# Loading a quarter of one weight chunk in two loads of 64 rows by the lower eight DMA engines, in a one-token attention kernel

## The chip, the cores and the metric

The kernel runs on one core of one Trainium2 chip. The time is the device time of one execution in microseconds (us), as the median of several runs. Most runs of one kernel agree within 0.3% (20 runs of the kernel before: 288.07 to 289.18 us, median 288.77). Now and then an execution takes some per cent longer (one of the changed kernel's took 297.79 us); such runs, the slow state, are left out of the ratios.

Engines are named as in the profile: PE (TensorE matmul), PEld (its weight load), DVE (VectorE), ACT (ScalarE), POOL (GpSimd), SP (SyncE, which issues nearly all transfers here). Beside them are 16 DMA engines. The traces do not number them. "Lower" is the name for the eight that carry a load whose source has an outer dimension of 8, "upper" for the other eight.

## The reference

One token goes through attention with a cached window and then a gated MLP. Cut to what matters here:

```python
x: (1, 1, 640)   k_cache, v_cache: (1, 32, 32768, 192)   wq: (640, 6144)   wo: (6144, 640)
W = 4096                                  # the last 4096 keys of each of 32 heads
q = layernorm(x) @ wq                     # 32 heads of 192
scores = q . k[:, :, -W:, :] / sqrt(192); p = softmax(scores); o = p @ v[:, :, -W:, :]
h  = x + o @ wo
h2 = h + mlp(layernorm(h))                # w_in (640 x 1536), gelu, gate, w_out (768 x 640)
```

All data are bfloat16. Keys and values are 2 x 50 MB, wq and wo 7.9 MB each: 119 MB in all, each byte used once.

## The kernel before

All large transfers are issued from SP in one fixed order: wq (five chunks of 128 rows), then tiles of keys and values of 3 MB, wo in pieces of 960 KB in between, and last w_in (five chunks) and w_out (six). Six buffers hold wq and KV tiles; SP issues a transfer once its buffer is free. The parts that the change and the argument touch:

```python
wq_v = A_wq.rearrange("(c p i) n -> c p (i n)", c=DC, i=4)      # DC = 5 chunks of 128 rows x 6144
...
def dma_wq(i):
    t = kvp.tile([P, KVE], BF16, tag="kv", name="wq_t")
    for c in range(2 * i, min(2 * i + 2, DC)):
        load(t[:, (c % 2) * HD:(c % 2 + 1) * HD], wq_v[c])        # 128 partitions x 12 KB
    tiles[("wq", i)] = t
...
for gq in range(NP // 2):                     # 8 groups of 4 heads
    psv = sc_bank()[:, 0:2 * Dh] ...
    for c in range(DC):
        wc = wq_sb[c // 2][...]
        for a in range(2):
            nc.tensor.matmul(psv, lhsT=xn2[:, c, a, :], rhs=wc[:, gq, a, :, :], ...)
    nc.scalar.activation(out=q2[...], in_=psv, func=ACT.Copy, scale=scale)
free("kv", NWQ)                               # now the next transfers may be issued
```

One chunk of wq reaches 128 partitions from 32 source runs of 48 KB (four rows each), so each DMA engine moves two packets of 48 KB for it (the trace of the kernel before has 160 such packets for the five chunks).

## Time and profile before

| | before |
|---|---|
| median of 6 runs | 288.61 us (288.27 to 289.18) |
| span of the profiled run | 286.9 us |
| main DMA queue, share of 16 engines | 96.9% |
| PE, DVE busy | 63%, 53% |
| one 48 KB packet, median | 1.815 us |

The page of the kernel before: the DMA share and the rate in 40 slices of 7.2 us, then the queues (packets, MB, share of 16 engines' span).

```profile
span 286.9 us, 3349 instructions
DMA  8999999999999999999999999999999998999991
GB/s 315 425 425 425 439 441 432 414 436 440 434 439 432 434 432 439 397 436 439 439 439 434 432 439 439 400 439 432 432 428 465 439 425 373 453 439 413 429 368 45
q1 hardware_dynamic: 4202, 119.35, 96.9%
q8 instruction: 11, 0.18, 0.2%
```

The DMA engines are busy from the first slice to the last, at nearly one rate (a packet counts in the slice in which it starts, so single slices scatter). No compute engine is near that (PE 63%, DVE 53%). Beside the data, eleven 16 KB packets of instructions (0.95 to 1.04 us each in the packet records) run on the DMA engines.

The end of the chain of waits of the kernel before, that is of the work that ended last, followed back at each step to what it waited for (start us, us, what):

```profile
271.52 8.71 DMA w_in_sb<-in_B_w_in_dram
280.23 0.05 issue
280.27 0.50 PE sm_ps L461 x12
284.46 0.28 DVE o_sb L490
```

And PE's timeline there (start us, us, engine, line, operation, count; in brackets the idle time before it and what ended it):

```profile
275.67 0.90 PE L376 MATMUL attn_ps<-o_1961,wo_t 128*128 128x1 bf16 x30 [1.07 <-DMA wo_t<-in_A_wo_dram]
278.65 1.42 PE L461 MATMUL sm_ps<-hb_2005,w_in_sb 128*128 128x1 bf16 x48 [0.33 <-DVE st_2007 L457]
280.27 0.48 PE L461 MATMUL sm_ps<-hb_2005,w_in_sb 128*128 128x1 bf16 x12 [0.20 <-DMA w_in_sb<-in_B_w_in_dram]
```

The end of the kernel hangs on the landings of wo and w_in. A transfer has landed when the last of its 16 shares has, so it is the slowest of the 16 DMA engines that counts here (the last completion in the third row below, at 278.16, is the landing at 280.23 of the chain above, on another clock). The trace holds the time of each of the 16 completions. Three transfers of the kernel before, in us on a clock that starts with the first data packet (2.1 us behind the page's clock), first completion and then the 16 offsets from it:

```
wq, chunk 0     4.65 | .00 .04 .05 .12 .15 .17 .25 .26  .52 .55 .64 .65 .68 .75 .83 .87
k, tile 0      26.48 | .00 .03 .04 .05 .12 .15 .17 .26  .53 .55 .65 .66 .67 .75 .80 .82
w_in, chunk 4 274.65 | .00 .03 .03 .41 .61 .70 .71 .82 1.47 1.62 2.00 2.00 2.16 2.19 3.40 3.51
```

At the start there are two groups of eight. At the end two engines are 3.5 us behind the first, 1.2 us behind the third-last. The average engine is done at 276.00, the last at 278.16.

### The profile page before, as it was taken

The numbers are of one execution on the slowest core, as the hardware profiler recorded it, in microseconds if no ns is written. First come the engines' busy times: TensorE is split into PE (matmuls) and PEld (weight loads), VectorE is DVE, ScalarE is ACT, GpSimd is POOL, SyncE is SP. The second block draws the span as 40 slices with busy tenths as digits, with TensorE's granted clock in tenths as the row PEclk, the third lists the DMA queues.
The fourth block names the chain that finished last, engine by engine and source line by source line (L and its number), as shares of the span: only waits on it lengthen the run. The fifth ranks groups of instructions, "written<-read, shape, count | busy, mean of one in ns | idle before, by whom it ended". The sixth has DMA issues, their size and how long they took to land.

```text
span 286.9 us, 3349 instructions
## 1 busy us (share of the span) xinstructions
PE 181.3 (63%) x1432; PEld 82.6 (29%) x1432; DVE 152.6 (53%) x204; ACT 28.7 (10%) x103; POOL 2.4 (1%) x13
## 2 busy tenths in 40 slices
PE   1229947698387664957394737656394919954853
PEld 0004613334133221423142313322141303423552
DVE  6100088998383909292565629290838447922133
ACT  2001300111002010101010010201010100201300
POOL 3000000000000000000000000000000000000000
PEclk9999989999959796987979896979597796998575
DMA  8999999999999999999999999999999998999991
GB/s 315 425 425 425 439 441 432 414 436 440 434 439 432 434 432 439 397 436 439 439 439 434 432 439 439 400 439 432 432 428 465 439 425 373 453 439 413 429 368 45
DMA packets 4223, 119.56 MB, mean 417 GB/s; under 512 B 1007, under 2 KB 1008, under 8 KB 1456
## 3 DMA queue, kind: packets, MB, share of 16 engines
q1 hardware_dynamic: 4202, 119.35, 96.9%
q8 instruction: 11, 0.18, 0.2%
q14 instruction: 4, 0.03, 0.0%
q10 hardware_dynamic: 6, 0.00, 0.0%
HBM read 119.34 MB, written 0.00 MB: 416 GB/s over the span
## 4 chain that ended last, share of the span: by engine, by line
DMA 68%; PE 16%; DVE 13%; SPq 1%; issue 1%; ACT 0%
DMA k_t<-in_A_k_cache_dram 34%; DMA v_t<-in_A_v_cache_dram 24%; DVE k_t L277 10%; PE sc_ps L283 9%; DMA wq_t<-in_A_wq_dram 7%; PE sc_ps L251 5%; DMA w_in_sb<-in_B_w_in_dram 3%; DVE S L291 1%; SPq L60 1%; PE pv_143 L338 1%; PE sm_ps L306 0%; PE attn_ps L372 0%; PE sm_ps L479 0%; PE pv_145 L338 0%; PE sm_ps L359 0%
## 5 line engine op out<-in xcount | busy, mean ns | idle before, releaser
L283 PE MATMUL sc_ps<-k_t,ident_bf 128*128 128x512 bf16 x384 | 112.5, 456 | 59.6 <-DVE k_t L277 59.6
L277 DVE TENSOR_TENSOR k_t<-k_t,q_178 128x6144 bf16<-128x6144 bf16 x32 | 107.2, 3352 | 58.0 <-DMA k_t<-in_A_k_cache_dram 58.0
L283 PEld LDWEIGHTS <-ident_bf 128*128 128x128 bf16 x384 | 42.0, 113 | 119.1 <-issue 70.7
L251 PE MATMUL sc_ps<-wq_t,xn_122 128*128 128x384 bf16 x80 | 17.7, 384 | 13.3 <-DMA wq_t<-in_A_wq_dram 10.9
L291 DVE TENSOR_REDUCE S<-sc_ps 128x32 f32<-128x512 f32 x32 | 21.6, 676 | 1.3 <-PE sc_ps L283 1.3
L308 DVE TENSOR_TENSOR bias<-off,sm_ps 128x2 f32<-128x2 f32 x16 | 2.4, 152 | 24.5 <-PE sm_ps L306 24.5
L259 DVE TENSOR_SCALAR sp_f<-sm_ps 128x1 f32<-128x1 f32 x1 | 0.2, 159 | 28.4 <-PE sm_ps L257 28.4
L251 PEld LDWEIGHTS <-xn_122 128*128 128x128 bf16 x80 | 8.7, 110 | 21.9 <-issue 15.6
L314 ACT ACTIVATE E_119<-S,bias 128x64 bf16<-128x64 f32 x12 | 4.2, 360 | 71.9 <-DVE bias L308 71.9
L338 PE MATMUL pv_143<-v_t,E_121 128*4 128x384 bf16 x96 | 6.2, 388 | 4.8 <-DMA v_t<-in_A_v_cache_dram 4.8
L314 ACT ACTIVATE E_120<-S,bias 128x64 bf16<-128x64 f32 x10 | 3.5, 361 | 51.6 <-DVE bias L308 51.6
L314 ACT ACTIVATE E_121<-S,bias 128x64 bf16<-128x64 f32 x10 | 3.5, 360 | 50.4 <-DVE bias L308 50.4
L338 PE MATMUL pv_145<-v_t,E_119 128*4 128x384 bf16 (+1 forms) x128 | 5.7, 327 | 3.7 <-DMA v_t<-in_A_v_cache_dram 3.7
L338 PE MATMUL pv_145<-v_t,E_120 128*4 128x384 bf16 x96 | 4.9, 325 | 4.7 <-DMA v_t<-in_A_v_cache_dram 4.7
L306 PE MATMUL sm_ps<-gm,ones_f 1*128 1x2 f32 x32 | 6.3, 263 | 2.3 <-DVE gm L301 2.3
L338 PEld LDWEIGHTS <-E_119 128*4 128x4 bf16 (+1 forms) x224 | 4.9, 91 | 8.8 <-issue 7.1
L301 DVE TENSOR_REDUCE gm<-sm_ps 1x2 f32<-1x128 f32 x16 | 4.4, 276 | 5.6 <-PE sm_ps L299 5.4
L306 PEld LDWEIGHTS sm_ps<-gm,ones_f 1*128 1x128 f32 x32 | 4.9, 190 | 8.1 <-DVE gm L301 3.5
L253 ACT ACTIVATE q_178<-sc_ps 128x384 bf16<-128x384 f32 x8 | 3.9, 490 | 29.8 <-PE sc_ps L251 29.8
L338 PEld LDWEIGHTS <-E_121 128*4 128x4 bf16 x160 | 3.3, 87 | 11.5 <-issue 10.4
L338 PEld LDWEIGHTS <-E_120 128*4 128x4 bf16 x160 | 3.2, 82 | 8.8 <-issue 7.5
L299 PE MATMUL sm_ps<-ident_f,m 128*1 128x128 f32 x16 | 5.0, 310 | 0.0
(151 smaller groups left out, 94.7 us busy)
## 6 DMA issues: line engine op xcount, KB each, us to landing
k_t<-in_A_k_cache_dram SPq DMA_DIRECT2D x15, 3072.0 KB, 32.2
v_t<-in_A_v_cache_dram SPq DMA_DIRECT2D x15, 3072.0 KB, 40.3
wq_t<-in_A_wq_dram SPq DMA_DIRECT2D x5, 1536.0 KB, 14.3
wo_t<-in_A_wo_dram SPq DMA_DIRECT2D x8, 960.0 KB, 32.5
w_in_sb<-in_B_w_in_dram SPq DMA_DIRECT2D x5, 384.0 KB, 23.2
k_t<-in_A_k_cache_dram SPq DMA_DIRECT2D x1, 1536.0 KB
v_t<-in_A_v_cache_dram SPq DMA_DIRECT2D x1, 1536.0 KB
w_out_sb<-in_B_w_out_dram SPq DMA_DIRECT2D x6, 160.0 KB, 5.5
```

The source lines that it names most:

```text
L60: eng.add_instruction(mybir.InstDMACopy(name=nc.get_next_instruction_name(), mode="Copy", queue="qSPDynamicHW", ins=eng.lower_ap_dma(in_, ...
L251: nc.tensor.matmul(psv, lhsT=xn2[:, c, a, :], rhs=wc[:, gq, a, :, :], start=(c == 0 and a == 0), stop=(c == DC - 1 and a == 1))
L253: nc.scalar.activation(out=q2[:, 2 * gq:2 * gq + 2, :], in_=psv, func=ACT.Copy, scale=scale)
L277: nc.vector.tensor_tensor(out=kc, in0=kc, in1=q2[:, t:t + 1, :].to_broadcast([P, JC, Dh]), op=ALU.mult)
L283: nc.tensor.matmul(psv, lhsT=ident_bf[:], rhs=k3[:, ch * JC:(ch + 1) * JC, n * G:(n + 1) * G], start=(n == 0), stop=(n == NT - 1))
L291: nc.vector.tensor_reduce(out=S[:, ch * JC:(ch + 1) * JC], in_=st[t]["ps"][ch], axis=AX.X, op=ALU.add)
L299: nc.tensor.transpose(out=mT[0:1, 0:P], in_=m[:], identity=ident_f[:])
L301: nc.vector.tensor_reduce(out=gm[:], in_=mT[0:1, 0:P].rearrange("o (g a s) -> o a g s", a=2, s=2), axis=AX.XY, op=ALU.max)
L306: nc.tensor.matmul(nb[:, 0:2], lhsT=ones_f[0:1, :], rhs=gm[:], start=True, stop=True)
L308: nc.vector.tensor_tensor(out=bias[:], in0=off[:], in1=nb[:, 0:2], op=ALU.subtract)
L314: nc.scalar.activation(out=E[:, :, a], in_=S[:], func=ACT.Exp, bias=bias[:, a:a + 1], accum_out=zq[q][:, a, b:b + 1])
L338: nc.tensor.matmul(pv_tiles[t % 2][p0:p0 + 2 * step, 0:step * Dh], lhsT=E[:, j:j + step, :].rearrange("p j a -> p (j a)"), rhs=vt[:, j * D ...
```

## The change

Its intent follows from that last row: the engines do not finish together, and a transfer that runs on the lower eight alone moves work from the upper ones to them. For the last 128 rows of wq, columns of three quarters of the heads come as before on all 16 engines. The last quarter (3 KB of each row) comes in two loads of 64 rows, both to partitions 0 to 63, side by side. A source whose outer dimension is 8 keeps the load on 8 engines. The matmuls of those heads then contract twice over 64 rows.

```diff
+    QCUT = 6 * 4 * Dh
 ...
-            load(t[:, (c % 2) * HD:(c % 2 + 1) * HD], wq_v[c])
+            if c < DC - 1:
+                load(t[:, (c % 2) * HD:(c % 2 + 1) * HD], wq_v[c])
+            else:
+                rows = A_wq[c * P:(c + 1) * P]
+                load(t[:, 0:QCUT], rows[:, 0:QCUT])
+                for h in range(2):
+                    load(t[0:HALF, None, h * HD + QCUT:(h + 1) * HD],
+                         rows[h * HALF:(h + 1) * HALF, QCUT:HD].rearrange("(a b) n -> a b n", a=8))
 ...
-    xn2 = const.tile([P, DC, 2, P], BF16)
+    xn2 = const.tile([P, DC + 1, 2, P], BF16)
 ... (x's last 64 values are put on partitions 0 to 63 once more: one matmul, two DVE operations)
-        for c in range(DC):
+        split = gq * 4 * Dh >= QCUT
+        nchunk = DC + 1 if split else DC
+        for c in range(nchunk):
+            n = HALF if split and c >= DC - 1 else P
 ...
-                nc.tensor.matmul(psv, lhsT=xn2[:, c, a, :], rhs=wc[:, gq, a, :, :],
+                nc.tensor.matmul(psv, lhsT=xn2[0:n, c, a, :], rhs=wc[0:n, gq, a, :, :],
```

No byte is added. Added work: four matmuls of 0.2 us in the q stage (72 of them in a row took 14.42 us in the kernel before), one tiny matmul, two small DVE operations (0.57 us for both there), two issues on SP (0.59 us each at the median).

More of the change, by code (lines that the diff above doesn't have):

```diff
@@ L229 @@
         nc.tensor.matmul(xc_ps[:, c:c + 1], lhsT=x_row[0:1, c * P:(c + 1) * P], rhs=ones_bf[0:1, 0:1], start=True, stop=True)
+    nc.tensor.matmul(xc_ps[0:HALF, DC:DC + 1], lhsT=x_row[0:1, D - HALF:D], rhs=ones_bf[0:1, 0:1], start=True, stop=True)
     x_pc = const.tile([P, 2, DC + 1], F32)
@@ L237 @@
     nc.vector.tensor_scalar(out=rstd1[:], in0=ln_rstd16(ln_nvar(mean1)), scalar1=1.0 / 16, scalar2=None, op0=ALU.mult)
-    for a in range(2):
-        nc.vector.tensor_scalar(out=xn2[:, :, a, :].rearrange("p c (g a s) -> p c a g s", a=2, s=2)[:, :, a],
-                                in0=x_pc[:, 0, 0:DC, None, None].to_broadcast([P, DC, HALF // 2, 2]),
-                                scalar1=mean1[:, 0:1], scalar2=rstd1[:, 0:1], op0=ALU.subtract, op1=ALU.mult)
+    for c0, c1, src in ((0, DC, x_pc[:, 0, 0:DC]), (DC, DC + 1, xc_ps[0:HALF, DC:DC + 1])):
+        n = src.shape[0]
+        for a in range(2):
+            nc.vector.tensor_scalar(out=xn2[0:n, c0:c1, a, :].rearrange("p c (g a s) -> p c a g s", a=2, s=2)[:, :, a],
+                                    in0=src[:, :, None, None].to_broadcast([n, c1 - c0, HALF // 2, 2]),
+                                    scalar1=mean1[0:n, 0:1], scalar2=rstd1[0:n, 0:1], op0=ALU.subtract, op1=ALU.mult)
     q2 = const.tile([P, NP, Dh], BF16)
@@ L247 @@
         psv = ps[:, 0:2 * Dh].rearrange("p (r d) -> p r d", r=2)
-        for c in range(DC):
+        split = gq * 4 * Dh >= QCUT
+        nchunk = DC + 1 if split else DC
+        for c in range(nchunk):
+            n = HALF if split and c >= DC - 1 else P
             wc = wq_sb[c // 2][:, (c % 2) * HD:(c % 2 + 1) * HD].rearrange("p (q a r d) -> p q a r d", a=2, r=2, d=Dh)
             for a in range(2):
-                nc.tensor.matmul(psv, lhsT=xn2[:, c, a, :], rhs=wc[:, gq, a, :, :],
-                                 start=(c == 0 and a == 0), stop=(c == DC - 1 and a == 1))
+                nc.tensor.matmul(psv, lhsT=xn2[0:n, c, a, :], rhs=wc[0:n, gq, a, :, :],
+                                 start=(c == 0 and a == 0), stop=(c == nchunk - 1 and a == 1))
         nc.scalar.activation(out=q2[:, 2 * gq:2 * gq + 2, :], in_=psv, func=ACT.Copy, scale=scale)
```

## The prediction

> **What bounds the kernel.** The DMA. The page gives 119.35 MB on the main queue, 96.9% of 16 engines' span, and 425 to 440 GB/s in most slices; a 48 KB packet takes 1.815 us (27.1 GB/s per engine) at its median in the packet records. The pieces of DVE and PE in the chain of waits (36.6 to 73 us) are not the limit: KV tiles keep landing every 7.26 us through that stretch, because transfers were queued 30 to 40 us ahead (DMA issues table). So the time is: first packet (3.3 us), the slowest engine's stream, and a tail. The timeline shows the tail hanging on landings: wo at 275.67, last w_in chunk at 280.27, w_out at 282.64, end 286.9.
>
> **The hidden imbalance.** The 16 completions of each transfer in the trace are not together. On the first wq chunk they spread over 0.87 us, in two groups of eight (0 to 0.26, 0.52 to 0.87). From then on the spread grows in steps of 1.4 to 1.55 us, one engine at a time, each when one of the eleven 16 KB packets of the "instruction" queue runs (0.95 to 1.04 us each; page, part 3). [...] Following the offsets, six of the first eight hit the later group, two the earlier, and a second round hits two of the later group again. At the end (last w_in chunks) offsets are 0, .01, .02, .39, .60, .68, .70, .80, 1.46, 1.60, 1.99, 1.99, 2.17, 2.18, 3.40, 3.56 us: by my tracking the early group ends at 1.6 or less, and the two stragglers are of the later group. Every landing is paid at 3.5.
>
> **Which half is which.** [...] The two-byte load on the Activation queue starts exactly when a packet of an early-group engine ends[...]. I take early = lower eight.
>
> **The change.** No bytes added or removed. wq's last chunk loses a quarter on the upper engines (24 KB each), which the lower ones get. Packet times read from the trace are close to linear (6 KB 0.235, 12 KB 0.465, 48 KB 1.815), so I estimate 0.35 us for 9 KB, 0.12 for 3 KB. Upper: 8 x 0.35 against 2 x 1.815, -0.85 us. Lower: plus 16 x 0.12, +1.05 us. New finish: upper 3.5 - 0.85 = 2.65, lower 1.6 + 1.05 = 2.65. Balanced: each late landing comes about 0.8 us earlier, and so do w_in, w_out and wo.
>
> Added: four matmuls in the q stage (4 x 0.2 us), one small matmul, two DVE operations before wq has landed, two DMA issues (0.6 us each). The q stage ends at 36.6 us; the transfers it frees are needed near 43 us. All off the critical path.
>
> **Prediction.** 288.6 - 0.8 = about 287.9 us, 80% range 287.2 to 289.0. Within 2%: 0.98.
>
> **What would show it.** Right: last w_in landing near 279.4, completion spread at the end about 2.7 instead of 3.5, 3 KB packets near 0.12 us, tile spacing still 7.26 us, same tail after w_in. First wq landings: the later group comes first in the last chunk.
>
> **What would make it wrong.** Early group is not the lower half (+1 us instead); 3 KB packets slow because eight engines write one half of the partitions (+1 us or so); instruction fetches falling on other engines with the ten added PE instructions; the queue running dry once at start through more transfers in flight.

The sharing out was to gain 0.8 us, which from 288.6 us gives about 287.9 us.

## The result, and the profile after

| | before | after |
|---|---|---|
| median | 288.77 us (20 runs, 288.07 to 289.18) | 289.48 us (10 runs; one of them slow, 297.79) |
| ratio of fast runs | | 1.0035, 95% interval 1.0023 to 1.0046 |
| span of the profiled run | 286.9 us | 287.5 us |

Of the ten runs of the changed kernel the nine fast ones have a median of 289.47 us. Ratios here and below are the mean time of one kernel's fast runs over that of the other's in the same rounds, so they are not quite the ratio of the medians. The change costs 0.7 us by the medians (1.0 us by the ratio) where 0.8 us were to be gained, and the result lies above the stated range. The loss is small, but the interval of the ratio leaves 1 out.

The page of the kernel after, the same lines:

```profile
span 287.5 us, 3362 instructions
DMA  7999999999999999999999999999999998999991
GB/s 308 431 388 405 424 433 410 424 465 434 438 438 431 440 417 424 428 423 438 438 438 447 431 438 438 390 433 438 438 430 455 431 433 380 456 438 409 439 376 63
q1 hardware_dynamic: 4442, 119.35, 97.1%
q8 instruction: 11, 0.18, 0.2%
```

The same megabytes, 240 packets more. The DMA share shows no hole, but the rate does: slices 3 and 4 (14.4 to 28.8 us, when the last chunk of wq comes) have 388 and 405 GB/s where the kernel before had 425 and 425 (with each packet shared out by time over the slices, 411 and 385 against 433 and 434). The engines are busy there and slow. A busy share alone would have hidden this.

The end of the chain of waits, and PE's timeline, after:

```profile
271.89 8.81 DMA w_in_sb<-in_B_w_in_dram
280.70 0.05 issue
280.75 0.49 PE sm_ps L475 x12
284.93 0.28 DVE o_sb L504
```

```profile
276.04 0.90 PE L390 MATMUL attn_ps<-o_1970,wo_t 128*128 128x1 bf16 x30 [0.69 <-DMA wo_t<-in_A_wo_dram]
279.88 0.48 PE L475 MATMUL sm_ps<-hb_2014,w_in_sb 128*128 128x1 bf16 x12 [0.35 <-DMA w_in_sb<-in_B_w_in_dram]
280.75 0.48 PE L475 MATMUL sm_ps<-hb_2014,w_in_sb 128*128 128x1 bf16 x12 [0.38 <-DMA w_in_sb<-in_B_w_in_dram]
```

The tail still hangs on the last w_in chunk and is as long as before, but that chunk comes 0.48 us later (280.75 against 280.27). The 16 completions say what happened:

```
k, tile 0      27.16 | .00 .02 .21 .22 .38 .39 .39 .40  1.58 1.59 1.62 1.63 1.70 1.73 1.73 1.74
w_in, chunk 4 275.17 | .00 .20 1.48 1.57 1.64 1.70 1.78 1.86 1.89 2.24 2.34 3.09 3.10 3.37 3.38 3.46
```

Two numbers of such a row are worth taking: the mean of the 16 (how much DMA time has been spent) and the distance from the mean to the last (how badly it is shared out).

| last w_in chunk | mean of 16 | last | last minus mean |
|---|---|---|---|
| before | 276.00 | 278.16 | 2.16 |
| after | 277.24 | 278.63 | 1.39 |

The sharing got better by 0.77 us, about what was predicted. But every engine, on average, came 1.24 us later. That loss is already whole at the first tile of keys (mean of 16: 28.12 against 26.87), and 248 us later it is the same. So it arose in the last chunk of wq and the first packets of keys behind it, and in no other place. (How far two traces agree: the first run below, in which nothing is lost, repeats the means of the kernel before within 0.03 us and its last completion within 0.14.) The packet records of that stretch of the kernel after:

```
size     count   min    median  max (ns)   from .. to (us, data clock)
9216 B   128     345    347     455        15.2 .. 18.9    16 engines
3072 B   128     121    158     242        18.0 .. 21.0    lower 8 engines (inferred)
49152 B  first k packets of the upper 8:  2767 to 2905     18.4 .. 21.7    (usual: 1815)
```

The 3 KB packets begin at 121 ns, as estimated, and swing between 121 and 242. Meanwhile eight 48 KB packets, those of the upper engines, which do not take part in these loads at all (by the same inference), take 2767 to 2905 ns, about a microsecond more than usual. Twelve more k packets that start by 21.5 us take 1828 to 2292 ns. Taken over 16 engines, the excess of the 48 KB packets is 0.71 us, that of the 3 KB packets over 121 ns is 0.37, that of the 9 KB packets over 347 ns is 0.04; the sizes alone would give 0.11. That is 1.23 of the 1.25 us by which the mean of the first k tile came later: the packet records account for the loss, and more than half of it lies in packets of keys and not in the new small ones.

### The profile page after: what moved, and what is told of

The parts are those of the page before. It is cut to its first block, busy times and chain, and to the rows that moved or that the text cites. A ratio compares the mean times of both kernels' runs of the same rounds, so it can differ in the third digit from the quotient of the medians.

```text
span 287.5 us, 3362 instructions
## 1 busy us (share of the span) xinstructions
PE 180.7 (63%) x1437; PEld 82.6 (29%) x1437; DVE 152.7 (53%) x206; ACT 28.7 (10%) x103; POOL 2.6 (1%) x13
## 4 chain that ended last, share of the span: by engine, by line
DMA 78%; PE 15%; DVE 3%; SPq 2%; issue 0%; ACT 0%
DMA v_t<-in_A_v_cache_dram 35%; DMA k_t<-in_A_k_cache_dram 34%; PE sc_ps L297 7%; DMA wq_t<-in_A_wq_dram 6%; PE sc_ps L265 5%; DMA w_in_sb<-in_B_w_in_dram 3%; DVE k_t L291 2%; SPq L60 2%; PE pv_147 L352 1%; PE pv_145 L352 1%; PE sm_ps L320 0%; PE attn_ps L386 0%; PE sm_ps L493 0%; PE sm_ps L373 0%; PE sm_ps L208 0%
## 5 line engine op out<-in xcount | busy, mean ns | idle before, releaser
L297 PE MATMUL sc_ps<-k_t,ident_bf 128*128 128x512 bf16 x384 | 110.0, 447 | 61.6 <-DVE k_t L291 61.6
L297 PEld LDWEIGHTS <-ident_bf 128*128 128x128 bf16 x384 | 41.4, 111 | 120.4 <-issue 70.1
L265 PE MATMUL sc_ps<-wq_t,xn_124 128*128 128x384 bf16 (+1 forms) x84 | 18.2, 374 | 12.5 <-DMA wq_t<-in_A_wq_dram 10.2
L265 PEld LDWEIGHTS <-xn_124 128*128 128x128 bf16 (+1 forms) x84 | 8.7, 108 | 21.7 <-issue 15.4
L352 PE MATMUL pv_145<-v_t,E_123 128*4 128x384 bf16 x96 | 6.2, 388 | 3.7 <-DMA v_t<-in_A_v_cache_dram 3.7
L352 PE MATMUL pv_147<-v_t,E_122 128*4 128x384 bf16 x96 | 4.9, 325 | 4.9 <-DMA v_t<-in_A_v_cache_dram 4.9
L352 PE MATMUL pv_147<-v_t,E_123 128*4 128x384 bf16 x64 | 3.9, 372 | 3.9 <-DMA v_t<-in_A_v_cache_dram 3.9
```

The costliest lines, as they stand in the source:

```text
L265: nc.tensor.matmul(psv, lhsT=xn2[0:n, c, a, :], rhs=wc[0:n, gq, a, :, :], start=(c == 0 and a == 0), stop=(c == nchunk - 1 and a == 1))
L297: nc.tensor.matmul(psv, lhsT=ident_bf[:], rhs=k3[:, ch * JC:(ch + 1) * JC, n * G:(n + 1) * G], start=(n == 0), stop=(n == NT - 1))
L352: nc.tensor.matmul(pv_tiles[t % 2][p0:p0 + 2 * step, 0:step * Dh], lhsT=E[:, j:j + step, :].rearrange("p j a -> p (j a)"), rhs=vt[:, j * D ...
```

## The experiments

Theory P (place): with 64 rows over 8 engines each engine writes 8 partitions in a row, and then two engines write the same group of partitions at once and hold up each other and everyone. With 32 rows, 4 in a row for each, no two would. This is a hypothesis: which rows an engine gets and which partitions would form such a group is in no trace, and the texts below that speak of an engine's rows (dealt out along the outer dimension of the source) or of groups assume it. What the runs can show is whether the loss follows the place that is written and the number of rows.

Theory H (source): reading 3 KB pieces 12 KB apart, or eight engines reading sources at certain distances, is slow in itself.

| run | 3 KB packets, ns | k tile 0, mean of 16 | last w_in, mean / last | median, us | ratio to before (95%) |
|---|---|---|---|---|---|
| before | none | 26.87 | 276.00 / 278.16 | 288.66 | 1 |
| after (the change) | 121 to 242 | 28.12 | 277.24 / 278.63 | 289.48 | 1.0035 (1.0023, 1.0046) |
| 3 KB pieces, all 16 engines | 121 | 26.86 | 275.97 / 278.02 | 289.01 | 1.0011 (0.9998, 1.0024) |
| rows dealt in turn | 121 to 221 | 28.20 | 277.32 / 278.75 | 290.38 | 1.0047 (1.0033, 1.0060) |
| four loads of 32 rows | 121 | 27.00 | 276.17 / 277.62 | 288.24 | 0.9994 (0.9981, 1.0007) |
| the same again | 121 | 26.90 | 276.10 / 277.48 | 288.18 | 0.9985 (0.9972, 0.9998) |
| 32 rows, every second partition | 121 to 159 | 27.47 | 276.59 / 279.11 | 289.39 | 1.0020 (1.0005, 1.0034) |

(The medians of the kernel before were 288.61 to 288.77 in the various rounds. The median of the run with rows dealt in turn holds one slow run, 294.42; its five fast ones have 290.33.)

### Is it the small pieces? All 16 engines, nothing doubled

```diff
-                for h in range(2):
-                    load(t[0:HALF, None, h * HD + QCUT:(h + 1) * HD], rows[h * HALF:(h + 1) * HALF, QCUT:HD]...)
+                load(t[:, QCUT:HD], rows[:, QCUT:HD])
-        split = gq * 4 * Dh >= QCUT
+        split = False
```

> The quarter of the rows is loaded as one piece of 3 KB for each of 128 partitions, by all 16 engines; nothing is doubled, and the compute is the one of before. Seen so far: in the changed kernel all 16 engines lose about 1.2 us on average while the 3 KB pieces run (the packet records show 0.12 to 0.24 us for one, and 2.8 us in place of 1.8 for the upper engines' first k packets). Theory P (two lower engines write into the same group of partitions at once, 8 rows in a row for each, and hold up everyone): no loss here, 3 KB packets 0.12 us, 288.8 us, ratio 1.000. Theory H (reading 3 KB pieces at a 12 KB step out of memory is slow in itself): the loss stays, 3 KB packets near 0.2 us, ratio about 1.003.

All 128 packets of 3 KB took 121 ns, and the mean at the first k tile is that of the kernel before (26.86 against 26.87). Small pieces at a 12 KB step are not slow. The form of theory H that blames them falls. The time is that of the kernel before within its interval.

### Is it the distance between the sources? Rows dealt to the engines in turn

```diff
-                         rows[h * HALF:(h + 1) * HALF, QCUT:HD].rearrange("(a b) n -> a b n", a=8))
+                         rows[h * HALF:(h + 1) * HALF, QCUT:HD].rearrange("(b a) n -> a b n", a=8))
```

> The same two loads by the lower 8 engines, with the same places written, but the rows are dealt out to the engines in turn[...] in place of 8 rows in a row. Gives a wrong result on purpose: the rows of the weights lie on other partitions than x. Theory P: the destinations are the same, so 3 KB packets stay between 0.12 and 0.24 us and the time stays at that of the change, ratio to before 1.003. Theory H with the distance between the engines' source rows (96 KB apart in the change, 12 KB here) as its cause: packets go to 0.12 us and the time to about 287.9, ratio 0.997.

If rows are dealt out as assumed, the sources of neighbouring engines are now 12 KB apart in place of 96 KB; the destinations are the same, and the loss is the same: 121 to 221 ns, mean at the first k tile 28.20. (The weights of the quarter lie on wrong partitions on purpose. The comparison with the reference accepted the result all the same, here and in the run with every second partition, so on this output it is no sharp test of that quarter.) The time is 0.3% to 0.6% above that of the kernel before where 0.3% was expected: three of the five fast runs took 290.3 to 290.4 us, two 289.4, the traced one among them. The second form of theory H falls.

### Is it the destination? Four loads of 32 rows

```diff
-                for h in range(2):
-                    load(t[0:HALF, None, h * HD + QCUT:(h + 1) * HD],
-                         rows[h * HALF:(h + 1) * HALF, QCUT:HD].rearrange("(a b) n -> a b n", a=8))
+                for h in range(2):
+                    for u in range(2):
+                        r0 = h * HALF + 32 * u
+                        load(t[32 * u:32 * u + 32, None, h * HD + QCUT:(h + 1) * HD],
+                             rows[r0:r0 + 32, QCUT:HD].rearrange("(a b) n -> a b n", a=8))
```

> The same bytes for the same lower 8 engines and to the same places, but in four loads of 32 rows, so each engine writes 4 rows at a time[...]. Theory P: 3 KB packets 0.12 us, upper engines' first k packets 1.8 us, the average loss of 1.2 us is gone, last w_in landing about 0.7 us earlier than before, 287.9 us, ratio 0.997. Theory H: as the change, 289.5 us, ratio 1.003.

Same bytes, eight engines again, same final places, but each engine gets four rows per load. All 3 KB packets take 121 ns, no k packet after them is slow, and the mean loss falls from 1.24 to 0.17 us. The last w_in chunk lands 0.54 us before that of the kernel before. The median is 288.24 against 288.66; the interval of the ratio still includes 1, because two of the six runs took 288.80 and 289.42, and the expected 287.9 us (0.997) was not reached. The run was repeated with the later ones.

### Isolating the place: whole rows by the lower eight, in two loads and in four

The kernel before, with the last chunk of wq loaded whole by the lower eight engines, so that packets are 12 KB and the sources are read whole:

```diff
-            load(t[:, (c % 2) * HD:(c % 2 + 1) * HD], wq_v[c])
+            ... for c == DC - 1:
+                for h in range(2):
+                    load(t[h * HALF:(h + 1) * HALF, None, 0:HD],
+                         rows[h * HALF:(h + 1) * HALF].rearrange("(a b) n -> a b n", a=8))
```

> The kernel of before, but the last 128 rows of wq come whole, in two loads of 64 rows, by the lower 8 engines alone, 8 rows of 12 KB in a row for each engine (16 packets each). Result right. The skew of about 7 us between the halves makes it slower; what is asked is the packet time. Theory P: 12 KB packets take up to twice the 0.465 us that the trace of before has for this size, and the upper engines' k packets are slowed beside them. Theory H: 0.465 us, as the rows are read whole.

and the same with `for h in range(4)` and 32 rows a load:

> The mate of the run in which the last 128 rows come whole by the lower 8 engines: now in four loads of 32 rows, 4 rows of 12 KB for each engine, same source pieces, same places. There the 12 KB packets took 0.46 to 1.41 us, 1.06 on average, and the upper engines' 48 KB packets up to 5.2 us. Theory P: no two of the lower engines share a group of partitions now. For rows 0 to 63 packets go to 0.465 us. For rows 64 to 127 the lower engines write into the partitions that the upper engines write at the same time (k), so there each of the two gets about half: 12 KB packets near 0.93 us, and the upper engines' 48 KB packets slowed to about twice, no more than 3.7 us. Rival (loads by 8 engines are slow whatever they write): as in the run with 64 rows.

These are single runs (302.27 and 295.65 us; both halves of the engines are far apart on purpose). The views of the stretches of time, columns: stretch, its length, busy PE, PEld, DVE, ACT, POOL, granted clock, DMA share, GB/s. The first stretch is the one in which the lower engines write partitions 0 to 63 in the run with 32 rows, the second the one in which they write 64 to 127. First two loads of 64 rows, then four of 32:

```profile
17.20:21.20 4.00, 0.80 (x2) 0.10 (x1) 0.00 (x0) 0.00 (x0) 0.00 (x0) 1.00 0.97 224
21.20:28.20 7.00, 0.00 (x0) 0.10 (x1) 0.00 (x0) 0.00 (x0) 0.00 (x0) 1.00 1.14 202
```

```profile
17.20:21.20 4.00, 0.80 (x2) 0.10 (x1) 0.00 (x0) 0.00 (x0) 0.00 (x0) 1.00 1.00 418
21.20:28.20 7.00, 0.00 (x0) 0.00 (x0) 0.00 (x0) 0.00 (x0) 0.00 (x0) 1.00 1.12 260
```

In the first stretch the lower engines of both runs write to partitions 0 to 63 alone, out of the same rows, and all engines are busy (DMA share 0.97 and 1.00). The run with 8 rows for each engine moves little more than half as much (224 against 418 GB/s; the view counts a packet whole in the stretch in which it starts, which is also how a share can pass 1; shared out by time it is 255 against 426). The packet records, in ns, show it in steps of one:

```
                               rows 0 to 63           rows 64 to 127
                               to partitions 0..63    to partitions 64..127
four loads of 32 rows          460, all 64            460 to 575 at the first, then 742 to 978
two loads of 64 rows           460 to 718 at first,   873 to 1411, mostly above 1100
                               then 741 to 975
upper engines' 48 KB packets beside them (usual: 1815):
four loads of 32 rows          1815 to 2080           mostly 3290 to 3782
two loads of 64 rows           3520 to 3569           4946 to 5231 at most
```

With 4 rows for each engine a 12 KB packet to partitions 0 to 63 took 460 ns. To partitions 64 to 127 it took 742 to 978 ns after the first ones, about twice as much, as expected (the upper ones' 3.78 us is slightly over the 3.7 us that was set). With 8 rows for each engine it took 741 to 975 ns even on partitions 0 to 63 after the first ones: about twice 460 again. And on partitions 64 to 127 it took 873 to 1411 ns, mostly above 1100, up to three times 460. Theory P reads these steps as one, two and three engines on a group of partitions, if the upper engines write their keys to partitions 64 to 127. The steps fit it; the sharing itself is in no trace. Both runs read the same rows whole. (At one time the engines' rows are 96 KB apart in the one and 48 KB in the other; the run with rows dealt in turn is the test of that distance.)

One thing goes beyond it. In the run with two loads the upper engines needed 3520 to 3569 ns for a packet while the lower ones wrote only to partitions 0 to 63. In the run with four loads they were at 1815 to 2080 ns at that time. If the upper engines write to partitions 64 to 127 alone, the lower ones held them up without sharing a place with them. In what way was not shown.

### Back again: 32 rows, but every second partition

```diff
-                        load(t[32 * u:32 * u + 32, None, h * HD + QCUT:(h + 1) * HD],
+                        load(t[u:HALF:2, None, h * HD + QCUT:(h + 1) * HD],
```

> As the four loads of 32 rows, with the same source rows for each engine, but written to every second partition of 0 to 63, so an engine's four rows lie in the same eight partitions as in the change[...]. Wrong result on purpose (rows on other partitions than x). Theory P: the loss comes back: 3 KB packets up to 0.24 us, slow k packets on the upper engines, about 289.4 us, ratio 1.003. Rival (a load by 8 engines is only harmful in pieces of 8 rows for each engine, or when its sources lie 96 or 12 KB apart): 121 ns and about 288.2, as with the four loads.

The sources of each engine are those of the four loads; only the destination changed, and the loss came back, somewhat under half of it: 3 KB packets 121 to 159 ns, 16 of the k packets beside them slowed (1976 to 2372 ns), the mean at the first k tile 0.5 to 0.6 us later than in the four loads. So the destination by itself brings a loss, and it is not the number of loads. That it is half as large was not predicted, and why was not shown. Nor was it tested whether writing every second partition is slow by itself, whichever engines write. That the time hit the expected 289.4 us is luck: in the profiled run (289.65) one straggler came over 1 us late for another reason, told below, and of the other three one took as long and two took 288.93 and 289.13.

### How much to shift: an eighth, a quarter, three eighths

The four loads with `QCUT` at 7, 6 and 5 of 8 groups of heads. The quarter was run once more beside them:

> The four loads of 32 rows for a quarter once more, to narrow the interval and as the mate of the other sizes on this chip: 288.2 us, ratio 0.998, last w_in landing 0.5 us earlier than before.

> Four loads of 32 rows for an eighth of the heads in place of a quarter: half the shift (12 KB for each engine). If the gain is the balance: no slow packets, the gap between the groups after wq about 0.4 us smaller than with a quarter, and the last w_in landing between before and the quarter: the stragglers of the upper half come 0.4 us earlier than before in place of 0.8; 288.4 us, ratio 0.999.

> Three eighths of the heads: 36 KB for each engine. With a quarter the last landings were 3.4 to 3.5 us (upper engines hit twice by an instruction packet) and 3.1 to 3.2 us (lower engines hit once) after the first. Half as much again moves the upper ones 0.4 us forward and the lower ones 0.5 us back, so now the lower ones come last, about as late: 288.1 to 288.5 us, no better than a quarter.

| share of heads | last w_in, mean / last | median, us | ratio to before (95%) |
|---|---|---|---|
| none (before) | 276.00 / 278.16 | 288.66 | 1 |
| an eighth | 276.04 / 277.71 | 288.35 | 0.9994 (0.9981, 1.0007) |
| a quarter | 276.10 / 277.48 | 288.18 | 0.9985 (0.9972, 0.9998) |
| three eighths | 276.08 / 279.15 | 289.66 | 1.0019 (1.0004, 1.0034) |

In none of them is a k packet slowed, and the means agree within 0.1 us: what differs is the sharing out alone. The last w_in chunk comes 0.45 us earlier with an eighth, 0.68 with a quarter. The chain of waits of the quarter:

```profile
270.64 8.93 DMA w_in_sb<-in_B_w_in_dram
279.61 0.49 PE sm_ps L477 x12
283.80 0.28 DVE o_sb L506
```

279.61 against 280.27 before and 280.75 in the change as it was given. This is the best version: it beats both kernels, the one before by 0.15% by the second ratio and by 0.06% by the first, whose interval includes 1. It is a small gain at the edge of what these runs can show, and the eighth is within their noise of it.

Three eighths missed its expectation. Its last engine was 5.5 us behind the first where the expectation comes to about 4 (3.1 + 0.4 + 0.5). The rows of completions show how: the instruction packet at 272.6 us (data clock) fell on an engine of the now later, lower group that had been hit once already (its offset went from 4.00 to 5.69 us). In the kernel before and in the change the packet at that time fell on an engine of the upper group. (Groups are followed by their offsets from row to row; the trace does not number the engines.) The same happened at that time in the run with every second partition (the last offset went from 3.20 to 4.56 us). Which engine is hit varies, so a plan that leaves just enough room for the lower engines is a gamble. The run times of three eighths lie in two bunches, two at 288.4 to 288.7 and four at 289.6 to 289.7, as this would have it; only one run of each kernel has a trace, so the link from bunch to hit was not shown.

### Do the instruction packets make the stragglers?

The kernel before with 512 one-element matmuls more on PE, which depend on no transfer:

```diff
+        if k_on:
+            dummy = bank()
+            for i in range(32):
+                nc.tensor.matmul(dummy[0:1, i:i + 1], lhsT=ident_bf[:, 0:1], rhs=ident_bf[:, 0:1], start=True, stop=True)
```

> The kernel of before with 512 idle one-element matmuls more on PE (32 in each of 16 steps, a weight load with each: 1024 instructions), which read nothing that is loaded and whose results nobody reads. It asks whether the 16 KB instruction packets make the stragglers. If they do: 15 instruction packets in place of 11, the 16 completions of the last w_in chunk on average about 4 x 1.45 / 16 = 0.36 us later against the first landing than in the kernel before, with more of them above 1.9 us (more than 8 of 16), and the time about 0.3 to 1.5 us longer, 289 to 290 us. If the stragglers have another cause: 16 completions spread as before, and 288.7 us.

The queues of that run:

```profile
q1 hardware_dynamic: 4202, 119.35, 96.9%
q8 instruction: 15, 0.25, 0.3%
```

```
w_in, chunk 4 274.44 | .00 .15 .15 .44 .75 .80 1.02 1.07 1.57 2.49 3.22 3.55 4.00 4.21 4.27 4.28
```

Four packets more, the mean of the 16 completions 0.44 us later (276.44). It was 0.09 us later already at the first k tile, before any instruction packet ran, so 0.35 us came after it, where 0.36 was expected. (Against the first landing, as the expectation has it, the mean is 0.65 us later, 2.00 in place of 1.35.) The spread is 4.3 us in place of 3.5, the last w_in landing 0.56 us later, the span 287.5. That agrees with the instruction packets as the cause of the spread. Two parts of the expectation missed: 7 of 16 offsets are above 1.9 us (6 in the kernel before), not more than 8, and the time was 288.85 us, ratio 1.0005 (0.9992 to 1.0019), less than the 0.3 us that had been set as the least. The traced run is longer by 0.6 us (at 289.29 it is the slowest of five), the other four hardly.

The traces also show most of how a packet of 1.0 us can set an engine back by 1.5: after seven of the eleven instruction packets of the kernel before, the 48 KB packet that starts as they end takes 2276 to 2324 ns in place of 1815.

## Why the prediction was wrong, point by point

- **DMA bounds the kernel, and the tail hangs on landings: right.** The chain ends in the w_in landing in the trace of every kernel but that of the four loads of whole rows, where it passes through a landing of wo, and the end moved with it: 280.75 and 287.5 after, 280.27 and 286.9 before.
- **Early group is the lower half, that is, the eight that carry the small loads: right.** The eight early engines of the k tile became the late ones. Taken by group means, the distance went from 0.58 us on one side to 1.41 us on the other, 1.99 in all; the estimate was 0.85 + 1.05 = 1.90. The runs in which no k packet was slowed are the clean test: with an eighth, a quarter and three eighths the distance at the first k tile is 0.41, 1.36 and 2.25 us, where shifting the lower group back from 0.58 us ahead by 0.95, 1.90 and 2.85 gives 0.37, 1.32 and 2.27. Had the early group been the upper half, the distance would have grown from 0.58 upward.
- **Better sharing worth about 0.8 us: right.** Last minus mean went from 2.16 to 1.39 us. But "completion spread about 2.7 instead of 3.5" was wrong (3.46): two upper engines now finish very early, since they were never hit. Distance from the mean was the quantity to predict, not the spread.
- **The step that failed: "I estimate 0.35 us for 9 KB, 0.12 for 3 KB. Upper: -0.85 us. Lower: plus 16 x 0.12, +1.05 us."** The term assumes that a packet takes what its size takes, and that the lower engines' load leaves the upper ones alone. The 3 KB packets took 0.167 us on average, up to 0.242, and the upper engines lost a microsecond in their next packets; the packets of keys beside the new loads cost 0.71 us of the mean, the 3 KB packets 0.37. The mean over 16 engines rose by 1.24 us where the estimate gave 0.1 us. The four loads of 32 rows, in which the estimate's packet times hold exactly (121 ns), gave what the prediction had promised for the change within 0.1 to 0.3 us: the last w_in landing 0.54 and 0.68 us earlier. (The timed gain was smaller: 0.42 and 0.48 us by the medians, 0.2 and 0.4 by the ratios.)
- **"3 KB packets slow because eight engines write one half of the partitions (+1 us or so)"** stood under what would make it wrong. That is close to what happened. Eight engines on one half do no harm by themselves, though: in the four loads they write the same half without loss (121 ns for 3 KB, and 460 ns for 12 KB in the four loads of whole rows). The harm came with eight rows for each engine, or with four on every second partition. That two engines then meet on a group of partitions is theory P's reading; it fits the steps of the whole-row runs, but neither the groups nor the way from there to the upper engines was shown.
- **Tile spacing 7.26 us, q stage off the critical path, DMA queue never dry: right.** The first three KV tiles of the kernel after land 7.24 to 7.25 us apart from 27.16 on, PE's last q matmuls start at 36.2 us in both kernels, and at least 14 packets were in flight whenever the records of the kernel after were sampled, every 50 ns from 6 to 270 us.

## What to carry to other kernels

When a DMA is split over few engines, try how many rows each gets and where they are written: on partitions 0 to 63, 12 KB packets took 460 ns with four rows for each of eight engines and up to 975 ns with eight, where the 48 KB packets of the other eight engines took 3.5 us in place of 1.8. When a kernel is bound by DMA, take the 16 completions of a transfer, and treat their mean (work, slow packets) and the last minus the mean (sharing out) as two separate sums; this change won one and lost more on the other. A busy DMA share says nothing about a slowed engine (in slices 3 and 4 the digit was 9 in both kernels, at 388 and 405 GB/s after against 425 and 425 before), so look at packet times and GB/s of the stretch that was touched.
